# The second batch of a block-sparse attention computed from gathered blocks instead of densely under a mask

## The chip, the cores and the metric

The kernel runs on one core of a Trainium2 chip. The metric is device time in microseconds (us). A core has TensorE (PE: matrix products; its weight loads are shown apart as PEld), VectorE (DVE), ScalarE (ACT), GpSimd (POOL) and SyncE (SP), which each work through a queue of their own in order, and 16 DMA engines. Products land in PSUM, all other tiles lie in SBUF.

## The reference

Four batches of attention with a block mask, and behind it a feed-forward layer with squared ReLU:

```python
batch, n_heads, seq, head_dim = (4, 8, 768, 64)      # block = 32, so 24 blocks a sequence
mask = |block_q - block_k| <= 1, or either block is 0 or 23
for qb in range(24):                                  # and 3 drawn key blocks for each query block
    for kb in sampled_blocks[qb]:
        mask[qb*32:(qb+1)*32, kb*32:(kb+1)*32] = True
attn = softmax(where(mask, q @ k.T / 8, -1e9))
x = attn @ v                                          # laid out as 3072 tokens x 512
r = maximum(x @ w_in, 0)                              # w_in: 512 x 2048
out = (r * r) @ w_out                                 # w_out: 2048 x 512
```

A query block in the middle thus sees at most 8 of the 24 key blocks (3 neighbours, the 2 edges, 3 drawn); the blocks 0 and 23 see all. The draw is an input, so which blocks to fetch is only known on the chip.

## The kernel before

**Two ways of attention.** `ND = 2` batches are computed densely, the other two from gathered blocks. A batch is handled as four head pairs (`u` is the number of a pair over all batches).

*Dense* (`scores`, `exps`, `masks`, `values`, `normalize`): for 128 or 256 queries of a head pair and two chunks of 128 keys, TensorE makes the transposed scores (L500; the two heads in the two halves of the array's rows), ACT takes the exponential into `pT` (L511), DVE multiplies by the 0/1 mask `MK` (L518), TensorE multiplies with the values (L540; a column of ones beside the values gives the sums). DVE divides (L548, L550) and TensorE transposes the result (L557) into `xT`, the input of the feed-forward. In batch 0 the first two tiles add the mask on TensorE instead (L504).

*Gathered* (`attend_sparse`): a tile is four query blocks (`blocks_of`), six tiles a batch; the last one has two ordinary blocks and the two edge blocks, which need all keys. For a tile DVE and ACT copy the window keys (`k_window`, by the helper of L281/L283), DVE copies the drawn key blocks (`k_random`, L667, with block numbers read into registers) and, in the first two tiles, the edge keys (`k_global`) into a key buffer `KG`; `q_tile` lays out the queries in `QG`. Values are rows of eight heads: `vd_write` (L635) writes a whole batch's values to `vd` in DRAM, and from there SP loads the windows (`v_window`, L693) and edges (`v_global`, L699) and POOL the drawn blocks by indirect DMAs (`v_random`, L703, one for each query block) into a value buffer `VG`. There are two buffers of each. Then `s_scores` (L715, L720), `s_exps` (L727), a patch that zeroes doubled columns in the edge tiles (`s_patch`), `s_values` (L761, in the array's mode of 32 columns), `s_normalize` (L769, L771) and `s_transp` (L777). The indices are worked out by some twenty small DVE instructions (`blocks_index`, L597 to L615).

**Loads and transposes.** `load` (L298, L300) fetches the float32 queries, keys and values of a pair into a raw set; casts to bfloat16 (`cast_qk`, `cast_v`, by L281/L283) follow. In batch 0 TensorE transposes queries and keys (L452), later pairs by DMA transposes on SP (L460). Batches 0 and 1 use four raw sets; later batches alternate between two, since the others become `KG` and `VG`. The pairs of batch 1 are loaded when the weights' last parts have landed (`loads_gate`).

**Feed-forward** (`hidden` L810, `relu` L819/L821, `square` L830/L832, `output` L860, `store`): in tiles of 128 and 256 tokens in batch 0 and of 384 in the others, two of the 16 strips of the hidden layer at a time. Both weights stay in SBUF.

**What sets the order.** Every step is a task with engines, costs, dependencies, buffers and a due time; `run_schedule` plans the tasks on all engines when the program is built, and its choice is the order of each engine's instructions. Numbers such as `TILE_AT` (the earliest time of each gathered tile), `EARLY` (of loads), `VISITS`, `TIES` and `SEEDS` (how ties fall) are settings of the planner. TensorE's queue thus mixes attention visits with feed-forward products, and it waits in order at whatever has not arrived. PSUM is three pairs of banks (`X`) for scores and hidden tiles, and two single banks for results.

Of the kernel before, what the change touches and what calls it, by code (L numbers as in the profile page):

```python
# [19 lines left out]
P = 128  # L20
# [5 lines left out]
def kernel(  # L26
# [30 lines left out]
    VS = D + 2  # L57
    ND = 2
# [6 lines left out]
    PT_BUFS, R_BUFS, G_BUFS, XT_BUFS = 6, 3, 17, 3  # L65
# [25 lines left out]
    AHEAD = {"PE": 0, "DVE": 0.11, "ACT": 0.133, "POOL": 0.0, "SP": 0.0}  # L91
    LEAD = -4.526
    NB_, SLEAD, KACT = 57.24, 3.669, 0.3
    EARLY = (60.677, -457.475, -41.207, 99.851, 111.859, -299.236, 123.361, 163.123)
    TILE_AT = (-39.154, 113.4, 58.045, 129.983, 53.984, 59.934, 133.038, 189.532, 195.761, 204.838, 216.885, 221.32)
    VISITS = (-22.52, -36.055, -56.543, -6.102, -38.911, -117.509, -11.957, -113.731, -113.459, -42.009, -41.809, -15.971, -8.974, 14.761, -119.048, -28.685, -131.348, -38.196)
    HOLD, PATIENCE = 0, 41.826
    PACE0, PACE, SINGLE, MASK_AT = 41.845, 1.392, 1, 17.0
# [5 lines left out]
    class Buf:  # L104
        def __init__(self, pool):
# [5 lines left out]
    TIES = 1.517, 3.165  # L111
    SEEDS = (
            182650, 593969, 290590, 139974, 165502, 836910, 587028, 462825, 164807,
            44065, 742728, 631950, 856096, 866859, 967498, 142637, 119601, 999059,
            76967, 598481, 340055, 172830, 184254, 4320)
# [178 lines left out]
    def load(u, e=None):  # L294
        b, a = divmod(u, HP)
        for w in range(3):
            if b < ND:
                sy.dma_start(out=raw[u][w].rearrange("p t n d -> p t (n d)"), in_=(qv, kv, vv)[w][b, a])  # L298
            else:
                sy.dma_start(out=raw[u][w].rearrange("p t (c n) d -> p (t c) (n d)", n=2), in_=sv[w][b][:, 2 * CP * a:2 * CP * (a + 1)])  # L300
# [79 lines left out]
    al = consts.tile([nb, n_rand + 1, nb], F32, name="al")  # L380
# [31 lines left out]
    VG = [flat[1][:, 0:8 * H * VS], MK.rearrange("p n s -> p (n s)")[:, 0:8 * H * VS]]  # L412
# [42 lines left out]
    def evac(u, w, ns, e):  # L455
        copy(e, QK[u][:, w].rearrange("r (n p) -> r n p", p=P)[:, ns], ttile.pop((u, w, ns.start))[:, ns])

# [175 lines left out]
    def vd_write(b, e):  # L633
        vn = VN[b % 2]
        sy.dma_start(out=vd[b][0:S, :].rearrange("(c p n) d -> p c (n d)", p=P, n=2),  # L635
                     in_=vn.rearrange("p (c n) h d -> p c (n h d)", n=2))
# [71 lines left out]
    def s_scores(b, t, x, s_, buf, e):  # L708
# [3 lines left out]
        for a in s_:  # L712
# [5 lines left out]
            for c in range(NCH) if n < 4 else ():  # L718
                w = 2 * (4 - n) * block
                nc.tensor.matmul(ps[:, at:at + w], QKB[b % 2][:, a, 1, c * P:(c + 1) * P], QG[x][:, a, :, :, n * 16:].rearrange("p h n (i m) -> p i h n m", m=16),  # L720
# [18 lines left out]
    def s_values(b, t, x, slots, buf, e):  # L739
# [5 lines left out]
        for s_ in slots:  # L745
            pT = spt.pop((b, t, s_))
            w = (2 * n + (NCH * (4 - n) if n < 4 else 0)) * block
            for j, a in enumerate(s_):
                for h in range(2):
                    hd = 2 * a + h  # L750
                    for c in range(2 if n == 4 else NCH):
                        for i in range(4):
# [4 lines left out]
                            else:  # L757
                                at = 2 * (j * w + 2 * n * block + (c * (4 - n) + i - n) * block) + h * block
                                rhs, last = VN[b % 2][:, (c % (NCH // 2)) * 2 + c // (NCH // 2), hd, 0:VW], c == NCH - 1
# [31 lines left out]
    TILES += [(b, c0, S // 2) for b in range(1, B) for c0 in (0, S // 2)]  # L791
# [113 lines left out]
    def prepare(u):  # L905
# [7 lines left out]
        if u >= HP:  # L913
            g = gate[GATES[min(u - HP, len(GATES) - 1)]]
            sp = u >= ND * HP
            ld_t = T_(("SP", 1.6), s0 - 30, load, u, deps=old_r + [g], dma=4.5 if sp else 4.6,
                      after=EARLY[u - ND * HP] if sp else 0.0)
            at = dict(deps=[ld_t])
            for w in (1, 0):
# [34 lines left out]
    def attend(group, add):  # L954
# [8 lines left out]
        sc_all.append(sc)  # L963
        for i, a in enumerate(group):
# [31 lines left out]
    sp0, qz, k_first, v_first, k_last = [], [], [], [], []  # L996
    PLACES = {0: 1, 1: 3, 3: 5, 5: 6}

    def blocks_prepare():
        x = T_(("SP", 0.4), 300.0, blocks_load, after=30.0, dma=0.2)  # L1000
        lanes, steps = blocks_index()
        sp0.extend([x, Task(("POOL", 0.6), 300.0, lanes, after=28.0)])
        for f in steps:
            sp0.append(Task(("DVE", 0.43), 300.0, f, deps=sp0[0:1] + sp0[-1:], port=True, nop=2))
        qz.extend(T_(("POOL", 1.0), 300.0, q_zero, i, after=40.0, deps=kws) for i in range(2))
        zb = Buf("pT")
        x = T_(("DVE", 0.2), 300.0, zero_rows, 0, after=45.0, get=[zb])
# [4 lines left out]
    def attend_sparse(b):  # L1012
# [5 lines left out]
        wr = T_(("SP", 0.6), base - 5, vd_write, b, deps=vals + sp0, dma=2.2)  # L1018
        xs_first = True
        for p_ in range(NT):  # L1020
# [3 lines left out]
            x = seq % 2  # L1024
            s = base + p_ * NB_ / NT
            kb, vb = Buf("KG"), Buf("VG")
            over = {0: lambda: [y for u in range(ND * HP) if raw_set(u) == 2 for y in cv[u] + tr[u]], 1: lambda: []}[x]() if seq < 2 else []
            vover = ([y for u in range(ND * HP) if raw_set(u) == 3 for y in cv[u] + tr[u]] if x == 0 else mks) if seq < 2 else []
            deps = []
# [4 lines left out]
            k1 = T_({"DVE": 0.5, "ACT": 0.9}, s - 8, k_window, b, t, x, list(range(n))[:2], deps=keys + over + k_first[-1:], get=[kb],  # L1034
# [3 lines left out]
            if n > 2:  # L1038
                deps.append(T_({"DVE": 0.5, "ACT": 0.9}, s - 8, k_window, b, t, x, [2, 3], deps=[k1], port=True, nop=2, bias={"ACT": KACT}))
            if p_ < 2:  # L1040
                deps.append(T_(("DVE", 0.8 if p_ == 0 else 0.49), s - 8, k_global, b, x, p_ == 0, deps=[k1], port=True, nop=2))
# [3 lines left out]
            deps.append(T_({"DVE": 0.7, "POOL": 1.3}, s - 8, q_tile, b, t, x, deps=qrs + [k1] + qz, after=late - SLEAD, port=True, nop=2))  # L1045
            v1 = T_(("SP", 1.1), s - 8, v_window, b, t, x, deps=[wr] + vover + v_first[-1:], get=[vb], dma=0.38 * n, after=late - SLEAD)
            vdeps = [v1]
            v_first.append(v1)
            if p_ < 2:
                vdeps.append(T_(("SP", 1.8), s - 8, v_global, b, x, deps=[v1], dma=1.0))  # L1050
# [6 lines left out]
            for k_, grp in enumerate(groups):  # L1057
# [19 lines left out]
                for u in us:  # L1077
                    va_of[u].append(va)
# [133 lines left out]
```

## Time and profile before

| | us |
|---|---|
| median of 3 runs | 265.58 (264.31 to 266.99) |
| profiled execution, whole | 264.92 |
| its span from first to last instruction | 263.1 |
| PE busy in it | 251.6 |
| ACT busy | 198.7 |
| DVE busy | 154.0 |
| POOL busy | 138.8 |

Busy means that at least one instruction of an engine runs; matrix products overlap in the array, so the length of one in the profile (230 ns for a transpose) is longer than the distance to the next (56 ns). The chain of waits is the path that ended last, followed back; with an engine so full most of its pieces are TensorE's own. The table of stretches gives each engine's busy time between two points of the span. The time is spent as follows: to about 58 us batch 0 attends, from 63 to about 116 batch 1, from 122 to about 170 batch 2 and from 189 to about 237 batch 3, with the feed-forward of the batch before in between.

### The profile page before, as it was taken

What the parts mean: (1) busy time and instruction counts of PE and PEld (TensorE: products, weight loads), DVE (VectorE), ACT (ScalarE), POOL (GpSimd) and SP (SyncE); (2) the same over time, 40 slices, a digit from 0 to 9 for tenths busy, and PEclk for the clock granted to TensorE, in tenths of its full rate; (3) what the DMA queues carried; (4) which work ended last, traced back from release to release, by engine and by line L of the source; (5) the groups of instructions that cost most, each with busy time, mean ns of one, the idle gap of its engine ahead of it and who ended that gap; (6) DMA issues with size and microseconds to landing.
All of it is one profiled execution on the core that took longest, in us unless ns stands there. A gap on an engine that the chain in (4) does not pass through costs nothing.

```text
span 263.1 us, 8679 instructions
## 1 busy us (share of the span) xinstructions
PE 251.6 (96%) x3519; PEld 162.9 (62%) x3552; DVE 154.0 (59%) x452; ACT 198.7 (76%) x303; POOL 138.8 (53%) x175
## 2 busy tenths in 40 slices
PE   7999999999998899999999999999999899999994
PEld 5778866677575466566576666545665566655544
DVE  7797789999999988873555623136075435121000
ACT  3888979988989998889877897423985568945920
POOL 4390625424579700668977775631767477702610
PEclk9999999999999999999999999999999999999999
DMA  6999999999636964299956999967616546231012
GB/s 204 353 278 207 205 196 302 381 191 285 169 66 173 199 165 128 85 213 295 223 141 145 257 167 233 272 218 190 136 42 181 152 120 142 71 105 42 0 40 82
DMA packets 62992, 46.40 MB, mean 176 GB/s; under 512 B 22088, under 2 KB 57832, under 8 KB 62952
## 3 DMA queue, kind: packets, MB, share of 16 engines
q1 hardware_dynamic: 56072, 36.79, 54.1%
q0 software_dynamic: 6336, 8.66, 17.3%
q8 instruction: 28, 0.46, 0.7%
q10 hardware_dynamic: 544, 0.39, 0.5%
q14 instruction: 12, 0.10, 0.2%
HBM read 37.32 MB, written 7.98 MB: 172 GB/s over the span
## 4 chain that ended last, share of the span: by engine, by line
PE 63%; DVE 13%; DMA 9%; ACT 5%; issue 5%; POOL 3%; SPq 1%; POOLq 0%; DVEq 0%; ACTq 0%
PE py L860 21%; PE X L810 21%; DVE pT L518 8%; PE po L540 4%; PE X L500 4%; DMA RAW<-in_q_dram 3%; PE X L761 3%; PE X L715 3%; ACT pT L511 2%; PE F L810 2%; DMA RAW<-in_k_dram 2%; POOL MK L703 2%; DMA RAW<-vd,idx 2%; DMA MK<-vd,idx 2%; PE X L860 2%
## 5 line engine op out<-in xcount | busy, mean ns | idle before, releaser
L832 POOL TENSOR_TENSOR g<-r 128x384 bf16<-128x384 f32 (+1 forms) x55 | 51.2, 937 | 78.7 <-ACT r L819 63.4
L860 PE MATMUL py<-w_out_sb,g 128*128 128x512 bf16 (+2 forms) x351 | 85.2, 367 | 2.4 <-issue 0.9
L810 PE MATMUL X<-xT,w_in_sb 128*128 128x384 bf16 (+1 forms) x512 | 84.0, 313 | 0.0
L511 ACT ACTIVATE pT<-X 128x1024 bf16<-128x1024 f32 (+1 forms) x76 | 70.7, 979 | 9.1 <-PE X L500 6.3
L810 PEld LDWEIGHTS <-w_in_sb 128*128 128x128 bf16 x640 | 55.6, 98 | 28.1 <-issue 1.9
L819 ACT ACTIVATE r<-X 128x768 f32<-128x768 f32 (+1 forms) x61 | 46.2, 762 | 14.4 <-PE X L810 12.1
L860 PEld LDWEIGHTS <-g 128*128 128x128 bf16 x416 | 35.9, 98 | 29.6 <-issue 2.0
L518 DVE TENSOR_TENSOR pT<-pT,MK 128x1024 bf16<-128x1024 bf16 x60 | 49.3, 850 | 2.4 <-ACT pT L511 2.2
L830 ACT ACTIVATE g<-r 128x384 bf16<-128x384 f32 (+1 forms) x65 | 33.6, 540 | 1.3
L727 ACT ACTIVATE pT<-X 128x1024 bf16<-128x1024 f32 x28 | 27.2, 1028 | 8.0 <-PE X L715 8.0
L769 DVE RECIPROCAL rss<-X 128x8 f32<-128x8 f32 x12 | 2.5, 208 | 51.9 <-PE X L761 48.7
L540 PEld LDWEIGHTS <-pT 128*128 128x128 bf16 x576 | 22.5, 97 | 7.9 <-issue 3.6
L540 PE MATMUL po<-VN,pT 128*128 128x65 bf16 x576 | 24.8, 193 | 2.1 <-DVE xT L283 1.4
L703 POOL DMA_INDIRECT MK<-vd,idx x24 | 22.7, 948 | 6.9 <-issue 5.6
L500 PE MATMUL X<-QK 64*128 64x256 bf16 (+1 forms) x336 | 25.4, 257 | 0.1
L281 ACT COPY ys<-py 128x512 f32<-128x512 f32 (+1 forms) x17 | 9.9, 582 | 17.9 <-PE py L860 17.9
L703 POOL DMA_INDIRECT RAW<-vd,idx x20 | 19.1, 954 | 5.8 <-issue 5.0
L283 POOL CAST VN<-RAW 128x768 bf16<-128x768 f32 x15 | 15.5, 1033 | 11.8 <-DMA RAW<-in_v_dram 11.6
L500 PEld LDWEIGHTS <-QK 64*128 64x128 bf16 x336 | 13.6, 94 | 10.0 <-issue 6.3
L283 DVE CAST qc<-RAW 128x768 bf16<-128x768 f32 (+3 forms) x22 | 13.2, 624 | 1.8 <-DMA RAW<-in_q_dram 1.0
L283 POOL CAST qc<-RAW 128x768 bf16<-128x768 f32 (+1 forms) x13 | 13.0, 1009 | 1.6 <-DMA RAW<-in_q_dram 0.8
L761 PEld LDWEIGHTS <-pT 128*32 128x32 bf16 x896 | 9.3, 95 | 6.2 <-issue 6.1
(109 smaller groups left out, 255.7 us busy)
## 6 DMA issues: line engine op xcount, KB each, us to landing
RAW<-in_v_dram SPq DMA_DIRECT2D x16, 384.0 KB, 7.1
RAW<-in_k_dram SPq DMA_DIRECT2D x15, 384.0 KB, 5.2
out_dram<-ys SPq DMA_DIRECT2D x21, 256.0 KB, 2.2
RAW<-in_q_dram SPq DMA_DIRECT2D x12, 384.0 KB, 4.2
MK<-vd SPq DMA_DIRECT2D x12, 198.0 KB, 4.1
w_in_sb<-in_moe_w_in_dram POOLq DMA_DIRECT2D x4, 512.0 KB
w_out_sb<-in_moe_w_out_dram POOLq DMA_DIRECT2D x4, 512.0 KB, 17.2
vd<-VN SPq DMA_DIRECT2D x2, 792.0 KB, 3.9
```

The source lines that it names most:

```text
L283: (V if e == "DVE" else G).tensor_copy(out=out, in_=in_)
L500: nc.tensor.matmul(ps[:, h, j * w:(j + 1) * w], QK[i][hs, 1, ksl], QK[i][hs, 0, qsl], start=j == 0, stop=not add, skip_group_check=True)
L511: A.activation(out=pT[:, :, 0:n], in_=stile.pop(a)[:, :, 0:n], func=AF.Exp, scale=scale)
L518: V.tensor_tensor(out=pT, in0=pT, in1=m[:, None].broadcast_to([P, 2, len(cs), w]), op=AOP.mult)
L540: nc.tensor.matmul(po[:, qc, h, :], pT[:, h, j * w + qc * P:j * w + (qc + 1) * P], VT[i][:, n, h, 0:VW], start=(n == 0 and qc == 0 and h = ...
L703: G.indirect_dma_start(out=VG[x][0:96, i, 1, :], out_offset=None, in_=vd[b][:, :], in_offset=bass.IndirectOffsetOnAxis(ap=idx[:, n:n + 1], ...
L727: A.activation(out=pT, in_=stile.pop((b, t, s_)), func=AF.Exp, scale=scale)
L810: nc.tensor.matmul(htile[T, f][:, i], w_in_sb[:, kc, (f + i) * P:(f + i + 1) * P], xT[b][:, kc, c0:c0 + w], start=(kc == 0), stop=(kc == K ...
L819: A.activation(out=to, in_=src, func=AF.Relu)
L830: A.activation(out=g, in_=r, func=AF.Square)
L832: (G if e == "POOL" else V).tensor_mul(out=g, in0=r, in1=r)
L860: nc.tensor.matmul(ytile[T, i], gtile[T, f][:, ts * P:(ts + 1) * P], w_out_sb[:, f, cs[0]:cs[1]], start=(f == 0), stop=(f == NF - 1))
```

## The change

- `ND = 1`: batch 1 too goes the gathered way. Its queries and keys are transposed by TensorE (`transp_pe`, 12 transposes for a pair into a pair of banks, then two copies), not by DMA (`BY_PE = 2`). It loads into the two alternating raw sets.
- A third value buffer `VG2`; the tiles take the three in turn, so `v_global` fills edges in the first three tiles of a batch. In SBUF it takes the place of two squared tiles (`G_BUFS` 17 to 15), one `xT` (3 to 2) and the tile `al`, which now lies in `KG1`.
- The feed-forward tiles of batch 1 have 256 tokens.
- Value runs: the values of all pairs are loaded with six rows of a head in one run, and `vd_write` writes them with one run for each partition; the keys of the all-keys scores are picked to match. A value row is padded to 68 elements instead of 66.
- In the tile with two ordinary blocks the values come in one visit instead of two.
- The index steps and the zeroing of `QG` may start earlier, and the planner has other costs and settings.

```diff
-    VS = D + 2
-    ND = 2
+    VS = D + 4
+    ND = 1
+    BY_PE = 2
-    PT_BUFS, R_BUFS, G_BUFS, XT_BUFS = 6, 3, 17, 3
+    PT_BUFS, R_BUFS, G_BUFS, XT_BUFS = 6, 3, 15, 2
...
-            if b < ND:
+            if b < ND or w == 2:
...
-    VG = [flat[1][:, 0:8 * H * VS], MK.rearrange("p n s -> p (n s)")[:, 0:8 * H * VS]]
+    VG2 = consts.tile([P, 8 * H * VS], BF, name="VG2")
+    VG = [flat[1][:, 0:8 * H * VS], MK.rearrange("p n s -> p (n s)")[:, 0:8 * H * VS], VG2]
...
+    def transp_pe(u, buf, e):
+        pt = pair_of(buf).bitcast(BF).rearrange("p (w c) -> p w c", w=2)[:, :, 0:NCH * P].rearrange("p w (n i) -> p w n i", i=P)
+        for w in (1, 0):
+            src = cast.pop((u, w, 0))
+            for n in range(NCH):
+                nc.tensor.transpose(pt[:, w, n], src[:, n].rearrange("p t d -> p (t d)"), identb)
+        for w in range(2):
+            ttile[u, w, 0] = pt[:, w]
...
-        sy.dma_start(out=vd[b][0:S, :].rearrange("(c p n) d -> p c (n d)", p=P, n=2),
-                     in_=vn.rearrange("p (c n) h d -> p c (n h d)", n=2))
+        sy.dma_start(out=vd[b][0:S, :].rearrange("(p n) d -> p (n d)", n=NCH), in_=VN[b % 2].rearrange("p n h d -> p (n h d)"))
...
-    TILES += [(b, c0, S // 2) for b in range(1, B) for c0 in (0, S // 2)]
+    TILES += [(1, c0, QW) for c0 in range(0, S, QW)]
+    TILES += [(b, c0, S // 2) for b in range(2, B) for c0 in (0, S // 2)]
...
+            if ND * HP <= u < BY_PE * HP:
+                qcs = [Buf("qc"), Buf("qc")]
+                for w in (1, 0):
+                    tr[u].append(T_({"DVE": 0.55, "POOL": 1.0}, 101, cast_qk, u, w, ALL, bias={"POOL": 0.5}, get=[qcs[w]], port=True, **at))
+                hb = Buf("X2")
+                t = T_(("PE", 0.68), s0 - 10, transp_pe, u, hb, deps=tr[u] + old_s, get=[hb], put=qcs, mode=128, mm=12)
...
-            x = seq % 2
+            x, z = seq % 2, (0, 2, 1)[seq % 3]
...
-            if p_ < 2:
-                vdeps.append(T_(("SP", 1.8), s - 8, v_global, b, x, deps=[v1], dma=1.0))
+            if p_ < 3:
+                vdeps.append(T_(("SP", 1.8), s - 8, v_global, b, z, deps=[v1], dma=1.0))
...
-            groups = [pairs] if n == 4 else [pairs[0:2], pairs[2:4]]
+            groups = [pairs]
```

## The prediction

> **What bounds the kernel now.** I read the page first, then the table of stretches, the chain of waits in order of time, the groups by shape, and the landings of the transfers.
>
> ```profile
> PE 251.6 (96%) x3519; PEld 162.9 (62%) x3552; DVE 154.0 (59%) x452; ACT 198.7 (76%) x303; POOL 138.8 (53%) x175
> PEclk9999999999999999999999999999999999999999
> ```
>
> TensorE is busy for 251.6 of 263.1 us at the full clock. That is only a bound if the busy time is dense, so I ask in which stretch it is not (columns: stretch, then busy us of PE, PEld, DVE, ACT, POOL, clock, DMA share, GB/s):
>
> ```profile
> 40.00:58.00 18.00, 17.24 (x224) 11.57 (x225) 17.10 (x42) 16.77 (x25) 6.31 (x6) 1.00 1.07 300
> 58.00:80.00 22.00, 21.63 (x256) 15.50 (x257) 20.70 (x40) 19.52 (x29) 13.00 (x12) 1.00 0.68 167
> 80.00:117.00 37.00, 34.44 (x430) 21.37 (x435) 32.47 (x58) 33.32 (x45) 17.59 (x17) 1.00 0.64 159
> 117.00:175.00 58.00, 57.28 (x840) 35.01 (x847) 25.82 (x107) 44.96 (x78) 42.48 (x53) 1.00 0.96 215
> ```
>
> From 80 to 117, where the second batch attends densely, PE is idle 2.6 us while DVE is busy 88% and ACT 90%; the chain there runs through the mask products ("88.17 2.16 DVE pT L518 x2"). From 117 on, in the gathered batches, DVE has half its time free and PE idles 0.7 us in 58. So the kernel is TensorE work almost end to end: what it gains or loses is PE work, plus the few places where PE waits. The price of that work is in the chain of waits (start, length, what):
>
> ```profile
> 96.48 0.54 PE X L500 x8
> 97.03 0.54 PE py L860 x2
> 97.56 0.74 PE po L540 x24
> ...
> 229.15 0.93 PE X L715 x32
> ...
> 230.95 0.62 PE X L761 x64
> 231.57 0.16 issue
> ...
> 232.97 0.22 PE X L777 x4
> ```
>
> One visit of dense scores takes 0.54, and the two output products behind it 0.54 instead of the 0.43 they take elsewhere: 0.65 a visit. 24 dense values take 0.74, 0.031 each. A gathered tile of four blocks costs 0.93 + 0.78 + 0.22.
>
> **The change, part by part.**
> *TensorE, batch 1 (second batch).* Removed: 18 score visits x 0.65 = 11.7; 288 values x 0.031 = 8.9; 24 transposes of results, 1.3. Sum 21.9. Added: scores of five tiles x 0.93 and of the two-block tile (16 products of 64 columns at 0.029, 24 of 128 at 0.056, as in batches 2 and 3) 1.8, together 6.5; values 5 x 0.78 + 1.4 = 5.3; result transposes 6 x 0.22 = 1.3; transposes of queries and keys, 48. Those have a near row, the first batch's own: chain row "21.38 0.55 PE F L452 x8", start to start 0.056, so 48 x 0.06 = 2.9. Sum 16.0. A rule speaks against this part: the Trainium skill, "TensorE: Matmul & The Clock Gate", Part 4: PE-mode transpose, gives about 275 ns for such a transpose inside a kernel. By it the 48 cost 13.2 us and the whole PE gain of 5.9 turns into a loss of 4.4. Its figure is a latency; here the latency (L452: 230 ns mean) overlaps, and the row decides: 2.9.
> *Feed-forward in tiles of 256.* 192 products of 256 rows at 0.109 against 128 of 384 at 0.1625: 20.9 against 20.8, +0.1. ACT and POOL get 24 of 0.60 for 16 of 0.81 (relu) and 24 of 0.63 or 1.20 for 32 of 0.52 or 0.85 (squares): level. One values visit for the two-block tile instead of two in batches 2 and 3: -0.4.
> PE in all: -21.9 + 16.0 + 0.1 - 0.4 = **-6.2**.
>
> *DVE and ACT.* Away: 36 mask products (mean 0.85) = 30.6 on DVE, 36 exponentials of 1.02 = 36.8 on ACT. New: 14 exponentials of 1.03; 66 random key copies of 0.23 to 0.25, windows, queries and globals, some 24 us on DVE; eight evacuations of transposes at 0.55. All of this lies under PE except in one place, costed below. The 2.6 us of PE idle from 80 to 117 go with the mask products: **-2.6**. What is late next there is PE itself: ACT has about 1 us of work per us of PE only until the first gathered tile, then less.
> *Third buffer of values.* In batches 2 and 3 PE waits 0.5 and 0.2 us for landings of gathers (list of waits, L761): **-0.7**, at most.
> *POOL.* 22 more gathers at 0.95 plus 0.30 of gap = 27 us, on an engine 53% busy; a tile of four costs 5 us, while PE spends some 8 us of mixed work per tile. Lies beside. A second rule speaks against it: the skill, "SBUF — State Buffer", A bandwidth-pool intuition that's wrong, says that a transfer whose descriptors GpSimd writes takes some 3.1 us instead of 0.62 beside a DVE copy, because DVE holds the shared port:
>
> ```profile
> L703 POOL DMA_INDIRECT MK<-vd,idx x24 | 22.7, 948 | 6.9 <-issue 5.6 <-PE py L860 0.3 <-PE X L715 0.3
> L667 DVE COPY KG<-QK 128x64 f32 x72 | 10.2, 228 | 0.5 <-issue 0.4
> L518 DVE TENSOR_TENSOR pT<-pT,MK 128x1024 bf16<-128x1024 bf16 x60 | 49.3, 850 | 2.4 <-ACT pT L511 2.2
> ```
>
> The 44 gathers of today run beside 132 such copies at a mean of 0.95: short copies hold the port shortly. By the rule a tile would take 13.6 us; I take 5.
> *DMA and SP.* Queries and keys of batch 1 come in runs of 512 B instead of 1,536, values in 1,536; eight DMA transposes leave SP; one more write of values (3.9 us to land) and six more tiles of window loads enter. No row separates the run lengths. Below: the eight transposes save SP some 11 us of issue; above: 1 us more per load, four times, on a chain that is costed next. I take zero. On SP the later loads of batch 2 now stand behind window loads that wait for a buffer's last values (third load issued near 90, fourth near 97, landing near 95 and 103); their keys are wanted near 120, so this is covered by some 10 us after casts and transposes.
> *The rest at nothing:* 15 instead of 17 squared tiles (a tile of 256 needs 8), two result tiles instead of three (batch 0's is read to the end before batch 2 writes its own, some 60 us later), the key order and the row padding change operands, not counts. Without that cover, one tile's wait for a buffer, about 1 us.
>
> *The hand-over, the one new wait.* In the order of the changed program TensorE meets the four query/key transposes of batch 1 between the last dense tiles. Each waits for casts, and behind each stand scores, values and feed-forward. Only two raw sets are left for loads, so the third pair's load is issued after the first pair's casts, the fourth's after the second's. From today's landings (first pair's values cast at 44.0, the next at 47.1 and 50.8, so 3.4 us a pair): third pair lands near 52.5, fourth near 56, and POOL casts it by 59. The cast of its keys or queries on DVE stands behind the last mask of batch 0. Today that mask ends at 57.97. DVE gets in front of it 15 more of the small index steps (0.2 us free, 0.45 as their mean today, since POOL holds the port for some of 0.8 to 1.0) = 3.0 to 6.8, three evacuations 1.7, and loses two output copies, a cast, a relu and a mask copy = 3.1: +1.6 to +5.4, of which its idle 1.2 us between 30 and 40 takes some. Ends: PE loses nothing, or 6 us (the upper end with a late cast of the first pair added). I take **+3.0**. After it the fourth transposes, their evacuation and six random copies need 6.3 us to the first gathered scores, and PE has 6.9 us of work in between: no further wait. Values: the write starts near 59, lands with a load in front of it near 63.5, windows and gathers near 72; PE asks for them near 78.
> For small waits that I can't place in the first gathered batch (it repeats what costs 0.5 to 1 us in the two others): **+0.8**.
>
> **Sum.** -6.2 - 2.6 - 0.7 + 3.0 + 0.8 = -5.7. The profiled execution took 264.92 (span 263.1 and 1.8 around it): 259.2. The median of the runs is 0.66 above it: 259.9, rounded to **260.0 us**.
>
> **Rivals.**
> 1. *The hand-over is long.* DVE and ACT are both over 90% busy from 40 to 80 today, and casts queue behind masks. If each of the two late loads also takes the 7.1 us that a values load takes in the median, the fourth transposes come 4 to 7 us later than I take: 264 to 267, so about 265, no change. For it: DVE 95% busy there. Against: lists show loads 3.4 us apart when queued.
> 2. *Slower: gathers starve.* Place: POOL, tile after tile of batch 1, with squares, casts and patches in the same queue. It decides from the point where a gather takes over 2.0 us (four in 8 us of PE). At the rule's 3.4 with gap, 13.6 us a tile, 5.6 behind on each of the five full tiles: +28, 288 us. Against: a mean of 0.95 us over all 44 of today.
> 3. *DVE's steps are free.* With index steps at 0.2 and no late cast the hand-over costs nothing and no small waits come: 256.2.
> 4. *The batch does not leave the path:* if PE's busy time were padded by waits, taking work away would give nothing: 265.6. Against: chain pieces give 0.216 a product of 512 rows at 1.00 of the clock, without padding.
>
> **How the numbers follow.** Forecast 0.62 (257 to 263), rival 3 0.11, rival 1 and 4 together 0.19, rival 2 0.08. The runs of before spread over 1.0%, so 1% is what can be told: below 262.9 is faster, above 268.2 slower. Forecast and rival 3 give 0.73, and the lower part of rival 1 adds 0.04: faster 0.77. Same 0.14, slower 0.09. For 8 in 10 I leave out rival 2 and the outer ends of 1 and 3: 256.0 to 265.0.
>
> **What would show it.** PE busy near 245 with its idle share no larger than 4%. L703 near 0.95 us with 66 gathers. The four groups of transposes of batch 1 on TensorE near 47, 52, 56 and 62, with idle time before them ended by DVE or POOL casts, some 3 us in all. Between 80 and 117 less than 1 us of PE idle. Wrong if gathers exceed 2 us, if the first gathered values wait for their landing, or if PE idles over 6 us from 40 to 75.

## The result: 279.3 us, 5% slower, and the profile after

The changed kernel takes 279.26 us in the median (277.61 to 280.03, four runs) beside 265.87 for the kernel before: a ratio of 1.051 (95% interval 1.047 to 1.054). 260.0 was predicted. Its profiled execution took 278.96 (span 277.2), 14.0 more than the one of before; the forecast for that execution was 259.2.

The head of the page after, and its clock row:

```profile
PE 256.7 (93%) x3880; PEld 172.4 (62%) x3880; DVE 143.2 (52%) x499; ACT 185.4 (67%) x304; POOL 154.1 (56%) x197
PEclk9999998699999799999979999999999999999999
```

PE is busy longer than before although it has less to do, and the clock row has three dips where before had none. The table of stretches (PE, PEld, DVE, ACT, POOL busy; clock, DMA share, GB/s), cut as in the prediction:

```profile
40.00:58.00 18.00, 14.86 (x173) 9.67 (x170) 14.36 (x35) 14.92 (x22) 7.98 (x8) 0.81 0.83 252
58.00:80.00 22.00, 20.71 (x230) 15.44 (x231) 18.14 (x59) 15.80 (x27) 11.83 (x14) 1.00 0.71 191
80.00:117.00 37.00, 33.99 (x718) 25.27 (x716) 17.88 (x71) 26.86 (x48) 27.20 (x36) 0.95 1.04 207
117.00:175.00 58.00, 54.76 (x858) 36.91 (x858) 31.16 (x122) 34.08 (x63) 37.95 (x44) 0.97 1.00 227
```

Before, PE idled 0.8, 0.4, 2.6 and 0.7 us in these stretches; now 3.1, 1.3, 3.0 and 3.2. ACT is emptier throughout and DVE up to 117, as the change meant, but PE doesn't use it. The groups:

```profile
L717 POOL DMA_INDIRECT MK<-vd,idx x24 | 22.1, 922 | 7.0 <-issue 6.6
L681 DVE COPY KG<-QK 128x64 f32 x108 | 14.6, 214 | 1.7 <-DVE QG L289 1.0
L534 DVE TENSOR_TENSOR pT<-pT,MK 128x1024 bf16<-128x1024 bf16 x24 | 21.7, 919 | 1.4 <-ACT r L834 0.8
```

Gathers take what they took before (0.92 us), beside more short copies on DVE: nothing starves there. The surprise is in the waits (engine, line, for whom: us in total, times, longest; "issue" is a wait for nothing that the profile shows), PE's first, POOL's next, and POOL's before the change last:

```profile
PE X L729 <- POOL QG L289: 3.4, 3, 2.4
PE X L791 <- issue: 2.2, 1, 2.2
...
PE X L775 <- DMA VG<-vd,idx: 1.3, 1, 1.3
```

```profile
POOL VN L289 <- DMA RAW<-in_v_dram: 13.2, 4, 5.2
POOL QG L289 <- DMA RAW<-vd,idx: 10.0, 3, 5.5
...
POOL QG L289 <- DMA MK<-vd,idx: 3.6, 1, 3.6
```

```profile
POOL VN L283 <- DMA RAW<-in_v_dram: 11.6, 6, 5.0
POOL QG L283 <- DMA RAW<-vd,idx: 3.1, 1, 3.1
```

The copies of gathered queries (QG) on POOL wait 13.6 us for landings of gathers, 3.1 us before the change, and PE's scores (L729) wait for them. The casts of values (VN) wait about as long as before. And the chain that ended last, in order of time (start, length, what), runs over POOL for 15 us:

```profile
222.44 0.91 DMA RAW<-vd,idx
...
223.40 0.60 POOL QG L289
...
225.99 0.62 POOL QG L289
...
226.87 0.93 POOL VG L717
...
235.40 0.91 POOL MK L717
...
236.38 0.83 POOL g L847
...
237.23 0.82 ACT r L834
...
238.10 0.48 PE X L825 x2
```

A landing, two query copies, eight gathers of 0.92 with 0.30 between them, a square, a relu, and only then PE, which had other work for most of that time and waits 0.7 us at its end. That is rival 2's queue, at a gather of 0.92 us.

To place the loss I add up, in the order of the program, each PE product at its own time (0.109 us for 256 rows, 0.217 for 512, 0.031 for a dense values product, and so on, from before's rows, with the gaps at a change of tile shape) and take the sum from the actual starts. What PE loses beyond its work, by stretch, good to about 1 us (the warm-up products of the last two rows are priced 1.7 us lower, though they took the same 3.1 us, so their first column is that much too high):

```
                       0-42  42-63  63-80  80-120  120-150  150-200  200-end   sum
before                  3.0    0.7    0.0     2.3      0.2     -0.8     -0.3   5.1
after                   3.3    8.0    0.3     4.6      4.0      2.2      3.4  25.8
queries on DVE          2.3    5.7   -0.1     4.2      4.7      0.8      0.2  17.8
no index steps          2.2    3.9    0.5     4.1      7.6      1.3      7.5  27.1
28 fewer                4.4    4.8    0.0     7.9      2.9      6.1      7.9  34.0
queries, 28 fewer       4.1    6.1    0.1     5.3      0.8      3.9      0.2  20.5
```

By these prices PE's own work fell by 6.3 us (254.5 to 248.2) and its losses grew by 20.7: +14.4, where 14.0 were measured. The lower rows are experiments below.

### The profile page after: what moved, and what is told of

It reads as the page before. It is cut to its first block, busy times and chain, and to the rows that moved or that the text cites. A ratio compares the mean times of both kernels' runs of the same rounds, so it can differ in the third digit from the quotient of the medians.

```text
span 277.2 us, 9541 instructions
## 1 busy us (share of the span) xinstructions
PE 256.7 (93%) x3880; PEld 172.4 (62%) x3880; DVE 143.2 (52%) x499; ACT 185.4 (67%) x304; POOL 154.1 (56%) x197
## 5 line engine op out<-in xcount | busy, mean ns | idle before, releaser
L825 PE MATMUL X<-xT,w_in_sb 128*128 128x256 bf16 (+1 forms) x576 | 89.8, 299 | 1.5 <-ACT QK L287 0.8
L847 POOL TENSOR_TENSOR g<-r 128x512 bf16<-128x512 f32 (+1 forms) x52 | 49.9, 963 | 54.8 <-ACT r L834 46.8
L834 ACT ACTIVATE r<-X 128x512 f32<-128x512 f32 (+1 forms) x62 | 43.0, 702 | 26.8 <-PE X L825 20.4
L741 ACT ACTIVATE pT<-X 128x1024 bf16<-128x1024 f32 x42 | 40.9, 1023 | 18.8 <-PE X L729 15.8
L527 ACT ACTIVATE pT<-X 128x1024 bf16<-128x1024 f32 (+1 forms) x40 | 35.5, 937 | 3.9 <-PE X L516 2.2
L717 POOL DMA_INDIRECT VG<-vd,idx x24 | 22.4, 932 | 6.5 <-issue 4.9
L534 DVE TENSOR_TENSOR pT<-pT,MK 128x1024 bf16<-128x1024 bf16 x24 | 21.7, 919 | 1.4 <-ACT r L834 0.8
L289 POOL CAST VN<-RAW 128x768 bf16<-128x768 f32 x15 | 13.7, 915 | 13.6 <-DMA RAW<-in_v_dram 13.2
L289 POOL COPY QG<-QK 64x512 bf16<-64x512 bf16 x12 | 7.6, 633 | 17.7 <-DMA RAW<-vd,idx 10.0
L289 DVE CAST qc<-RAW 128x768 bf16<-128x768 f32 (+3 forms) x25 | 16.1, 662 | 1.7 <-DMA RAW<-in_q_dram 0.9
L556 PE MATMUL po<-VN,pT 128*128 128x65 bf16 x288 | 13.6, 196 | 2.5 <-POOL VN L289 1.0
L681 DVE COPY KG<-QK 128x64 f32 x108 | 14.6, 214 | 1.7 <-DVE QG L289 1.0
L556 PEld LDWEIGHTS <-pT 128*128 128x128 bf16 x288 | 11.9, 99 | 5.5 <-issue 2.8
```

The costliest lines, as they stand in the source:

```text
L289: (V if e == "DVE" else G).tensor_copy(out=out, in_=in_)
L527: A.activation(out=pT[:, :, 0:n], in_=stile.pop(a)[:, :, 0:n], func=AF.Exp, scale=scale)
L534: V.tensor_tensor(out=pT, in0=pT, in1=m[:, None].broadcast_to([P, 2, len(cs), w]), op=AOP.mult)
L556: nc.tensor.matmul(po[:, qc, h, :], pT[:, h, j * w + qc * P:j * w + (qc + 1) * P], VT[i][:, n, h, 0:VW], start=(n == 0 and qc == 0 and h = ...
L681: V.tensor_copy(out=words(KG[x][:, :, i, 128 + 32 * j:160 + 32 * j]), in_=keys_of(b)[:, :, :, bass.ds(r, 8)])
L717: G.indirect_dma_start(out=VG[x][0:96, i, 1, :], out_offset=None, in_=vd[b][:, :], in_offset=bass.IndirectOffsetOnAxis(ap=idx[:, n:n + 1], ...
```

## The experiments

My theory after the result had four parts: POOL's query copies wait for landings; PE's instruction fetch stalls; the hand-over from 42 to 63 us is longer than I took; half-clock stretches follow these waits. The rival to each is that a removed wait is replaced by the next.

Ten of the eighteen runs fell on three chips that take 301 to 306 us for the kernel before, with pauses of some 0.67 us inside scores and values of small products from about 80 to 130 us on. Their times are compared only with others on the same chip, and of their traces only the first 75 us are used, except for the waits made on purpose further below. A wait named in the text without a view is counted from where the product before it should have been followed, which is up to 0.3 us more than the idle time in the views.

### Gathered queries on DVE

```diff
-            copy(e, QG[x][hs, :, h, :, 0:n], src[hs, :, :, m:m + n])
+            copy("DVE", QG[x][hs, :, h, :, 0:n], src[hs, :, :, m:m + n])
```
(and the same for the two-block tile's second copy)

> The changed kernel with one edit: the copies of gathered queries (L697, L699), which the schedule puts on POOL for five of the eighteen tiles, go to DVE at the same place in the order. Theory 'landings': on POOL the second of each pair of copies waits until every gather issued before it has landed (gaps of 2.5, 3.6, 5.5, 3.2 and 2.0 us ahead of it in the trace), and PE's scores wait behind it at 138.7 (2.57 us), 207.8 (0.82) and 226.0 (0.48); the wait at 138.7 also drops the granted clock to 0.5 for 3.4 us, worth 1.7. So 279.3 falls to about 274 (272.5 to 275.5) and the half-clock stretch at 141.7 is gone. Rival 'the next wait': late keys of batch 2 hold PE at the same place, and the time stays at 278 to 280. DVE gets 10 copies of about 0.25 us, which cost at most 0.5.

Measured: 270.72 us, ratio to before 1.021 (1.015 to 1.026): 8.5 below the changed kernel, more than expected. POOL in order of time around 131 to 146, first the changed kernel, then this one:

```profile
132.47 0.95 POOL L717 DMA_INDIRECT RAW<-vd,idx  x1
133.73 0.91 POOL L717 DMA_INDIRECT RAW<-vd,idx  x1 [0.30 <-issue]
134.64 0.62 POOL L289 COPY QG<-QK 64x512 bf16<-64x512 bf16 x1
140.73 0.61 POOL L289 COPY QG<-QK 64x512 bf16<-64x512 bf16 x1 [5.46 <-DMA RAW<-vd,idx]
...
143.52 0.95 POOL L717 DMA_INDIRECT VG<-vd,idx  x1 [0.15 <-issue]
```

```profile
131.47 0.95 POOL L717 DMA_INDIRECT RAW<-vd,idx  x1
132.72 0.93 POOL L717 DMA_INDIRECT RAW<-vd,idx  x1 [0.30 <-issue]
...
138.19 1.07 POOL L717 DMA_INDIRECT VG<-vd,idx  x1 [0.15 <-issue]
```

The second copy of the pair sits 5.46 us behind two gathers that have nothing to do with queries; without it the next gathers issue 5.3 us sooner. In the trace that second copy waits on the semaphores of four gathers, the two just issued among them. Part one is shown, but its size is less sure: of the 7.9 us between the profiled executions the table puts 4.7 behind 63 us, 1.0 ahead of 42 and 2.3 into 42 to 63, where the changed kernel's profiled execution had a stretch at half clock and this one had none. The first query copy on POOL stands at 73.7 us, so the 3.3 us ahead of it are not the copies' doing.

### No index steps on DVE

```diff
+        steps = [steps[3] if i == 3 else (lambda: None) for i in range(len(steps))]
         def lanes(e):
+            G.iota(idx, pattern=[[block, n]], base=0, channel_multiplier=1)
```

> The changed kernel with the index steps on DVE (L613 to L631) left out, but for the one that the key copies read; the gathers take fixed rows instead of the sampled blocks, so the random blocks of batches 1 to 3 get other values. Theory 'hand-over': seven index steps stand ahead of the reciprocal at 43.7 and start the row of PE waits at 43.0 (1.22 us), 44.9 (0.79) and 46.0 (0.79), after which the clock is granted at 0.5 for 6.8 us: without them some 2 us of waits and 2.5 to 3 us of half clock go, 279.3 falls to 274 to 276. Rival 'masks': what bounds this stretch are masks, exponentials and evacuations; the waits only move, and the time falls by 0 to 1 us.

Measured: 277.72, ratio 1.045 (1.039 to 1.050), some 1.5 us below the changed kernel, which is not clear of the noise (1.047 to 1.054); the profiled execution took 280.3. The stretch of the hand-over, in before, changed, queries on DVE, and this kernel:

```profile
42.00:63.00 21.00, 20.19 (x255) 14.74 (x255) 19.53 (x49) 18.99 (x29) 8.25 (x9) 1.00 1.06 289
```

```profile
42.00:63.00 21.00, 16.68 (x211) 11.31 (x208) 17.26 (x42) 15.67 (x22) 8.81 (x9) 0.84 0.76 227
```

```profile
42.00:63.00 21.00, 16.45 (x225) 12.20 (x223) 17.66 (x42) 17.78 (x25) 10.34 (x10) 1.00 0.87 270
```

```profile
42.00:63.00 21.00, 18.47 (x256) 13.82 (x255) 16.96 (x31) 19.55 (x28) 11.91 (x12) 1.00 0.90 284
```

Without the steps PE is busy 2.0 us more than in the kernel with the queries on DVE, which also has the full clock here. In all kernels below that run this stretch at the full clock PE is busy 16.1 to 17.7 us with the steps on DVE and 18.3 to 18.7 without: the steps' share is real, 0.6 to 2.6 of some 5 us. But by the table this kernel is 5.2 us ahead of the changed one at 63 us and 1.3 behind at the end. Among its waits the query copies have grown from 3.4 us to

```profile
PE X L732 <- POOL QG L289: 7.3, 3, 2.6
```

(at 135.6, 204.9 and 224.2). In this execution what is won ahead of POOL's queue is given back at it. It lies 2.6 us above the kernel's median, so how much is given back in general is not shown.

### Where the instruction blocks end

An instruction queue moves 30 packets of 16 KB (the page's row "q8 instruction: 30, 0.49, 0.8%"). PE has 7,760 products and weight loads and 41 semaphore instructions in the trace, 30.5 times 256, and the kernel before has 28 packets for 27.9 times 256 (33 products that its trace lacks counted in); so I take one packet as 256 of PE's instructions. PE in order of time where the wait of 2.2 us is put down to "issue":

```profile
86.66 0.33 PE L791 MATMUL X<-places,xs 128*128 128x128 bf16 x3
89.14 0.23 PE L791 MATMUL X<-places,xs 128*128 128x128 bf16 x1 [2.15 <-issue]
```

It stops between the third and fourth transpose of one tile; a packet of that queue runs from 86.47 to 87.67. The test moves all later instructions by splitting products of batch 0 (which leaves their hidden sums incomplete; the work is the same):

```diff
+            for x0, x1 in ((0, w // 2), (w // 2, w)) if split else ((0, w),):
-                nc.tensor.matmul(htile[T, f][:, i], w_in_sb[...], xT[b][:, kc, c0:c0 + w], ...)
+                nc.tensor.matmul(htile[T, f][:, i, x0:x1], w_in_sb[...], xT[b][:, kc, c0 + x0:c0 + x1], ...)
```

> The changed kernel with 32 of batch 0's hidden products (256 rows) written as two halves each: the same PE work to within 0.2 us, but every later PE instruction stands 64 places further back. Theory 'instruction fetch': some 6 to 8 us of PE's lost time are stalls where a block of 256 instructions is used up faster than the next one is fetched, and where the boundaries fall decides; from the order of the instructions, with 4.6 us from one fetch to the next, the stalls grow by 1.5 to 2 us: 279.3 becomes about 281 (280.5 to 282), and the gap of 2.3 us at 86.8 stands elsewhere or is gone. Rival 'chance': the gaps are waits for other engines that only happen to stand beside fetches, and time and gaps stay as they are, 279 to 279.8.

> The same with 96 products split, so that later PE instructions stand 192 places further back (64 ahead of a block's boundary), for at most 0.6 us more PE work. Theory 'instruction fetch': nearly all stalls at the three values visits of 128 products and behind them go (86.8, 150.6, 181.3, 211, 217.4), and with the first of them the half-clock stretch at 90.5: 279.3 falls to 270 to 274. Rival 'chance': 279.3 to 280.

Measured: 281.45 (1.060, 1.056 to 1.064) and 283.05 (1.064, 1.058 to 1.069). The first is as expected; the second is 9 to 13 us above what I had. Then fewer instructions ahead of everything, with and without the queries on DVE:

```diff
-    for _ in range(N_WARM):
-        nc.tensor.matmul(FB[1][:, 0:256], warm[:, 0:P], warm, start=True, stop=True)
+    for _ in range(N_WARM // 2):
+        nc.tensor.matmul(FB[1], warm[:, 0:P], warm[:, None, :].broadcast_to([P, 2, 256]), start=True, stop=True)
```
(and every second idle product left out, the others twice as wide)

> The kernel with the gathered queries copied on DVE, and 28 PE instructions fewer at its start (seven warm-up products of 512 rows in place of fourteen of 256, every second idle product left out and the others twice as wide). In three traces PE stops at its 2,492nd instruction or just not, whatever stands there (results' transposes in two, values in one, feed-forward in one), and later stops stand near multiples of 256 from it. Theory 'instruction fetch': with the boundaries moved by 28, no block of 256 is used up in less than 4.6 us any more (reckoned from the order and the starts in the trace with the queries on DVE), the stalls of 3.28, 1.44 and 0.41 us go, and the half-clock stretch behind the first with them: 270.7 becomes 264 to 266. Rival 'the next wait': PE meets a later wait instead, 268 to 270.5.

> The kernel with queries on DVE and 28 PE instructions fewer at its start, once more: the chip it ran on first took 301.7 us for the kernel before, with pauses of 0.67 us in a row inside values and scores of small products that no other trace here has, so that run tells little. Theory 'instruction fetch', as then: on a chip that runs the kernel before in 265 us it takes 264 to 266. Rival 'the next wait': 268 to 270.5.

> The changed kernel with the 28 PE instructions fewer alone (queries stay on POOL). Theory 'instruction fetch': the stops at 86.8 (2.32), 150.6 (about 1.4), 181.3 (1.51), 217.4 (1.46) and 237.1 (0.83) go, less what the landings on POOL's queue take back: 279.3 becomes 273 to 276. Rival: the time stays within 1 us of 279.3, since PE catches the same waits for landings later.

Measured: 273.23 us with the queries on DVE (1.028, 1.020 to 1.036), 2.5 above the kernel without this edit, and 282.55 without them (1.054, 1.044 to 1.063). The first try, on a chip at 301.7, gave 318.2 (1.054, 1.049 to 1.060). My forecasts of a gain all fell; the changes against the kernels without this edit, +2.5 and +3.3, are within the noise. The place of the stops held. These are PE's stops at "issue" of over 0.2 us idle in the nine kernels on the faster chips, by the number of the product or weight load in program order (number: us; then their sum and the time of that profiled execution); the kernel before has none:

```
changed               2,491: 2.32   5,543: 1.51                                 3.8   279.0
64 further back       959: 0.49     2,491: 4.50   4,781: 1.97   6,309: 1.30     8.3   279.3
192 further back      959: 0.41     1,215: 1.75   3,253: 1.88   5,035: 0.38     4.4   285.1
queries on DVE        2,491: 3.28   5,037: 0.38                                 3.7   271.0
no index steps        2,491: 2.03   2,743: 0.85                                 2.9   280.3
queries, 28 fewer     2,491: 1.02   3,507: 1.51   4,781: 2.11   5,545: 2.76     7.4   272.1
28 fewer              5,543: 3.17                                               3.2   285.6
loads moved (below)   5,545: 2.12                                               2.1   272.8
steps on POOL (below) 4,525: 0.86   5,033: 2.18   6,053: 2.30                   5.3   288.7
```

Three more stops, 0.2 to 0.35 us idle at 4,263, 4,269 and 4,275, are left out. With the semaphore instructions of PE's queue counted too, all 23 in the table have a number that leaves 193 or 194 when divided by 256 (2,498 and 5,569 in the changed kernel), whatever stands there: at 2,491 it is result transposes in three kernels, gathered values in one and output products in another. The three left out leave 186, 192 and 198. And in all 23 PE goes on 1.2 to 1.7 us after a packet of that queue has landed (after the three left out, 4.1 to 6.5), while in the changed kernel it comes to most of the other such numbers 2 to 15 us after the last packet. So the stop belongs to the instruction's number and ends with a packet: that PE waits for its instructions is shown. What such stops cost is not: sums of 3.8 and 8.3 us stand in executions of 279.0 and 279.3, 3.7 and 7.4 in 271.0 and 272.1. I had reckoned the stops from the order alone, with 4.6 us from one packet to the next, and that misjudged the later ones; the traces have packets 3.3 us apart (at 231.3 with the queries on DVE and 28 fewer). The kernels "192 further back" and "28 fewer" show that with the queries on POOL a smaller sum doesn't help. In the latter the chain of waits from 103.8 on is POOL's:

```profile
103.79 0.91 POOL VG L721
...
106.23 0.91 POOL VG L721
...
107.16 1.06 POOL g L851
...
108.24 0.60 ACT r L838
...
108.89 0.91 PE X L779 x64
```

Gathers, a square behind them, a relu, and PE's values after a wait of 4.9 us (this execution took 285.5, 3.0 above the kernel's median). A last try with 36 fewer (three idle products instead of seven) fell on two of the slower chips:

> Queries on DVE and 36 PE instructions fewer at the start (seven warm-up products of 512 rows, three idle products of 512). With 28 fewer PE still stopped, at instructions 3,507, 4,781 and 5,545 (1.5, 2.1 and 2.8 us), and these are the same instruction numbers at which other kernels here stop: seen from 2,491 the boundaries drift forward by some 18 in 3,000, so 28 were right for the first and too few for the later ones. Theory 'instruction fetch': with 36 none of the three is left at more than 0.5 us, and the time is 265 to 268. Rival 'the next wait': other waits of the same length stand in their place and the time stays at 270 to 273.

> Queries on DVE and 36 PE instructions fewer, once more, since the first try fell on a chip that takes 302 us for the kernel before. Theory 'instruction fetch': no stop of over 0.5 us at instructions near 3,507, 4,781 and 5,545, and the time is 265 to 268. Rival 'the next wait': 270 to 273.

316.1 us against 302.5 (1.043, 1.029 to 1.056) and 318.9 against 305.2 (1.032, 1.027 to 1.038). What a placement without any stop is worth stays open.

### Index steps left out where the queries are on DVE

The edits are those above, together.

> The same, and the index steps on DVE left out but for the one that the key copies read (gathers of fixed rows: random blocks of batches 1 to 3 get other values). Theory 'hand-over by index steps': the first waits of the row (1.5 and 0.8 us at 42 to 45) go and with them 1.5 to 3 us of the time with the steps. Rival 'masks and evacuations': the waits from 42 to 60 stay at 4 us or more in sum and the time is within 0.8 us of the one with the steps.

> The same without the index steps on DVE but for the one that the key copies read (random blocks of batches 1 to 3 get other values). With the queries on DVE nothing on POOL's queue should take the gain back later. Theory 'hand-over': from 42 to 63 PE loses some 5.5 us with the steps; without them 3.5 to 4, so the time is 1.5 to 2 us below that of the kernel with the steps. Rival: PE's loss there stays within 0.5 us of that with them, and so does the time.

> The same without the index steps on DVE (random blocks of batches 1 to 3 get other values), once more. Theory 'hand-over': 1.5 to 2 us below the kernel with the steps. Rival: within 0.5 us of it.

All three were on the slower chips: 315.4 (318.2 with the steps, same chip), 312.6 (316.1) and 317.5 (318.9). Each is lower, but the intervals of the ratio overlap in all three pairs, so no gain in time is shown. The stretch from 42 to 63, ahead of those chips' disturbance, repeats the finding; both with 36 fewer, with the steps and then without:

```profile
42.00:63.00 21.00, 16.80 (x233) 12.51 (x230) 19.09 (x42) 18.29 (x26) 10.28 (x11) 1.00 0.87 268
```

```profile
42.00:63.00 21.00, 18.65 (x261) 13.76 (x258) 16.90 (x30) 19.49 (x28) 11.62 (x11) 1.00 0.88 275
```

1.85 us. PE still idles 2.3 us there where it idled 0.8 before the change: five kinds of waits of 0.3 to 0.5 us each, for results of the dense tiles, casts and evacuations of the new transposes and a square on POOL.

### Loads on another queue, index steps on POOL

With the queries on DVE the chain of waits at 124 us shows a further candidate, the last keys of batch 2:

```profile
123.93 4.57 DMA QK<-qc
...
128.62 0.21 DVE RAW L686
...
128.87 0.34 ACT RAW L287
129.20 0.51 ACT KG L287 x2
```

```diff
+        eng_ = sc_ if u in (10, 11) else sy     # in load(u), for its three DMAs
```

> Queries on DVE, 28 instructions fewer, and the third and fourth load of batch 2 issued by ACT's queue in place of SP's. In the changed kernel's trace SP issues them at 97.8 and 114.6, behind windows that wait for a buffer and transposes that wait for casts, and the last keys of batch 2 land near 128.5, for which PE waits 2.1 and 0.7 us when nothing else holds it. Theory 'SP's order': the loads go out earlier, the waits near 127 to 131 go, and the time is 2 to 3 us below that of the kernel without this edit. Rival 'casts and write are late anyway': no change beyond 0.7 us.

> The same, and the index steps on POOL (maxima of flags as sums with a minimum behind them) in place of DVE. Theory 'hand-over by index steps': DVE's queue is free ahead of the reciprocal at 43.7 and PE waits some 1.5 us less from 42 to 46, so the time is 1 to 2 us below that of the kernel with the steps on DVE, and below the kernel before: 260 to 262. Rival 'POOL's casts': the steps stand ahead of the casts of values, queries and keys on POOL, take the shared port, and what is gained is given back: within 0.7 us, or slower.

Measured: 273.88 (1.035, 1.030 to 1.040), no gain over 273.23, and 290.44 (1.097, 1.093 to 1.101), 17 us worse. The first decides nothing on SP's order, for two reasons. The loads of batch 2 don't go out in the order of their pairs: `u` of 10 and 11 are the second and the fourth in time, so the load that SP issued at 97.8 stayed with SP, and the fourth went out at 110.9 on ACT's queue where SP had issued it at 109.1. And the kernel without this edit no longer has the waits near 127 to 131; with the queries on DVE alone, and then with 28 fewer too:

```profile
120.00:150.00 30.00, 26.72 (x461) 19.49 (x459) 16.93 (x78) 19.18 (x36) 17.83 (x22) 1.00 1.07 222
```

```profile
120.00:150.00 30.00, 29.74 (x500) 21.96 (x502) 18.26 (x83) 21.75 (x40) 19.40 (x23) 1.00 0.96 222
```

In the second (waits from 93 to 113):

```profile
ACT pT L748 <- issue: 12.5, 2, 12.2
POOL VN L289 <- DMA RAW<-in_v_dram: 6.5, 1, 6.5
PE X L832 <- ACT pT L748: 6.4, 1, 6.4
```

ACT's load needs the raw buffer that POOL's casts of the load before are still reading; they end between 107.0 and 108.5, the load issues from 107.8 to 109.8, and an exponential stands behind it for 12.2 us. The hand-over itself had gained (PE busy 18.27 of 21 from 42 to 63). A DMA on a computing engine's queue brought its wait with it here; what the late loads cost stays open.

### What a wait costs beyond itself

The kernel before, with four waits made on purpose, and with products in their place:

```diff
+        if (b, t) in ((2, 1), (2, 3), (3, 1), (3, 3)) and s_ == (0, 1):
+            for _ in range(1):      # 13 where the wait is replaced
+                nc.tensor.matmul(ps[:, 0:512], identb, w_in_sb[:, 0, 0:512], start=True, stop=True)
+            for _ in range(4):      # of w_in_sb[:, 0] where it is replaced
+                V.tensor_reduce(out=junk, in_=ps[:, 0:512], axis=AX.X, op=AOP.max)
```

> The kernel before, with PE made to wait at four places of batches 2 and 3 (one product into the scores' buffer, then four reductions of it on DVE, which the scores wait for): some 2.9 us each, 11.6 in all. Theory 'clock': each such wait drops the granted clock to 0.5 for one stretch of 3.41 us, which costs 1.7 us more, so the kernel is 15 to 19 us slower than before. Rival 'waits alone': no stretch at half clock or none that costs, 11 to 13 us.

> The kernel before, with thirteen products of 512 rows at the same four places in place of the waits (2.8 us each, 11.2 in all), and the four reductions beside them on DVE with nobody waiting. Both theories: 11 to 12 us slower than before, the clock at full speed throughout. What the kernel with the waits takes beyond this, less the difference of the waits and the products in the traces, is the price of the clock.

> The kernel before with four waits of PE of about 3.2 us each (measured on the other chip: 3.13, 3.19, 3.20, 3.98), 12.9 in all. Theory 'clock': each is followed by a stretch of 3.41 us at 0.5, 1.7 us each, so 17 to 20 us slower than before. Rival 'waits alone': 11 to 14 us slower, because the stretches fall on work that PE had to wait for anyway or don't come.

> The kernel before with thirteen products of 512 rows in place of each wait, 2.8 us each: 11 to 12 us slower by both theories, with the clock at full speed.

Both pairs fell on the slower chips: 314.95 against 312.15, and 314.25 against 312.51, that is 2.8 and 1.7 us more with the waits. The waits measure 13.5 and 12.8 us in the traces, with 4 x 0.216 for their own products 14.4 and 13.7; the replacement is 52 x 0.216 = 11.2. By these sums the waits should cost 3.2 and 2.5 us more, a little over what was measured. But the kernel with products has a wait of its own that the other lacks:

```profile
PE X L721 <- ACT pT L733: 4.3, 1, 4.3
```

(at 266.8 in the first pair, 4.2 us in the second), and nearly as many half-clock stretches (eight of 3.41 us in the first pair's trace) as the one with waits (nine); the intervals of the ratio overlap too. So the price of a stretch is not tested. What the faster chips say: four runs of the changed kernel with mean clocks of 0.975, 0.980, 0.982 and 0.994 took 279.0, 280.0, 279.6 and 277.6 us, and with the queries on DVE the one run at the full clock was the slowest of four (272.4). The stretches are real in their place, yet these times don't follow them.

## Why the prediction was wrong, step by step

*PE work, -6.2.* Right: -6.3 by the products' own times, a sum and not a measurement of its own. The transposes of queries and keys came at 0.055 us each (twelve from 55.26 to 55.87); row, not rule.

*POOL "lies beside".* The step that failed most. I multiplied 22 gathers by their duration and compared busy times. The duration held (0.92 to 0.93); what I put at nothing is what else stands in that in-order queue and waits: query copies for landings (13.6 us in place of 3.1), with gathers and squares behind them. Taking the query copies off gave 8.5 us, of which the traces place 4.7 where those copies stand. Value casts wait for loads too (13.2 us), but about as long before (11.6), and 22.0 in the faster kernel with the queries on DVE, so they are not the cause. Rival 2 named the place and had 8 in 100, but tied it to a gather over 2.0 us; here a copy's wait for landings of 2.0 to 5.5 us was enough. None of the three signs of being wrong that I had listed came: gathers at 0.92, PE idle 4.4 us from 40 to 80, no wait of the first gathered values. They did not look at this queue.

*The hand-over, +3.0.* Mechanism right, size short: 5.0 us over before with the queries on DVE (5.7 against 0.7), 0.6 to 2.6 of it by the index steps. The transposes came at 50, 55, 60 and 68 us, not 47, 52, 56 and 62. "No further wait" behind it held: 0.3 us from 63 to 80.

*PE idle from 80 to 117, -2.6, and third buffer, -0.7.* The mask waits did go, yet PE idles 3.0 us there: the stop at instruction 2,491 (2.3) and a wait at 110 stand there instead. Values still wait 1.3 us for a landing at 217. I took a vacated wait for a gain without asking what is next but PE.

*One values visit in place of two, -0.4.* It packs 128 products with as many weight loads, a whole block of instructions, into about 2 us. The longest stop stands behind or inside the first such visit in three kernels (2.3, 3.3, 4.5 us). That the merging itself causes it was not tried apart.

*Keys of batch 2 "covered by some 10 us".* Wrong: SP issued the third and fourth load at 97.8 and 114.6, not near 90 and 97, and with the queries on DVE the keys landed near 128.5. There PE loses 4.7 us from 120 to 150; with 28 instructions fewer it loses 0.8, with the fourth load no earlier than 109.1, so the price of this step stays open.

*"At the full clock".* I carried 1.00 over from before. The first two of the waits from 43 to 46, the stop at 86.8 and the wait at 138.7 were each followed by a stretch at 0.5, 13.7 us in all.

Together, for the kernel with queries on DVE: 12.2 us of losses over before's row and the forecast's terms are +2.0 in the hand-over, +3.6 from 63 to 120, +4.5 from 120 to 150, +2.8 behind, less 0.7 ahead. The change also took other planner settings, feed-forward tiles of 256 and longer value runs, and none of these was tried apart; how much of the 14 us is the order and not the gathered batch stays open. No version tried beats the kernel before; the nearest is 2% slower.

## What to carry to other kernels

An in-order queue is not costed by its busy share: list what in it waits for something slow (a landing, a load) and who stands behind that; one kind of copy moved to another engine was worth about as much as the whole batch's PE saving. A gain ahead of such a queue can be given back at it, so test a cause only after the later bound is taken away, and check in the trace that the edit moved what it was meant to move. And where a change makes a dense engine's instructions smaller and more, look at whether their supply keeps up.

## What was not expected of the hardware

PE stops of 0.4 to 4.5 us at the same place in a block of 256 instructions, put down to "issue" in the waits; each ends 1.2 to 1.7 us after a packet of 16 KB on the instruction queue. And the clock: stretches of 3.41 or 6.83 us at half speed followed pauses of 2.3 us, of 2.6 us, and two of 1.2 and 0.8 us within 3 us. The Trainium skill, "TensorE: Matmul & The Clock Gate", Part 1, has the clock fall to half after at least one idle window of about 3.4 us; the length agrees, but these pauses are shorter. Not every such pause has a stretch behind it: 2.8 us at 176.6 in the kernel with the queries on DVE and 28 fewer was followed by none, so what decides stays open. And chips differ: three of them took 14 to 15% longer for the same kernel, with 0.67 us pauses in small products, for which no run here gives a cause.
